# First MLP block of a fused attention and MLP kernel: from two halves of 256 columns to four token tiles of 128 columns

## The chip, the cores and the metric

One core of a Trainium2 chip. The metric is device time in microseconds (us) of one launch. Engines in the profile: PE (TensorE matmul; PEld its weight loads), DVE (VectorE), ACT (ScalarE), POOL (GpSimd), SP (SyncE, which here issues most DMAs).

## The reference

```python
def reference(A_x, A_wqkv, A_wo, B_x, B_w1, B_w3, B_w2):
    # _A_ref(x, wqkv, wo): q, k, v = x @ wqkv, 32 heads of 32; each position attends to
    #   itself and 7 earlier ones, 2 apart; softmax; then @ wo
    # _B_ref(x, w1, w3, w2): (silu(x @ w1) * (x @ w3)) @ w2
    x = A_x                       # 1 x 2048 x 1024, bfloat16
    xn = _layernorm(x, axis=-1)
    s = _A_ref(xn, A_wqkv, A_wo)  # wqkv 1024 x 3072, wo 1024 x 1024
    g = _silu(_B_ref(xn, B_w1, B_w3, B_w2))   # w1, w3 1024 x 3584, w2 3584 x 1024
    return x + s * g
```

## The kernel before

The 2048 tokens are worked in 4 chunks of 512 (`CH`), each chunk of 4 token tiles of 128. A chunk needs its normalized tokens transposed: `xnT`, 128 partitions x 8 (`KT`, the slices of D) x 512 tokens. With `xnT` as the moving operand, the weights being the stationary one, PE makes gate and up of 14 blocks of 256 features (`w1`, `w3` tiles of 512 KB each), q, k and v, and then multiplies by `w2` and `wo`. DVE does the windowed attention beside this in pieces that the list `side` hands out with estimated costs. The schedule is manual: each engine's instructions stand in the order in which the code issues them, and each engine's queue is worked in that order.

The change is in the start of chunk 0 (lines 524 to 598), where no earlier work covers the normalization. Tiles of tokens are `x0[0..3]`. The loads of tiles 0 and 1 come in halves from SP and ACT (L112, L113), those of 2 and 3 from SP (L115), then six weight tiles (`load_w`, L167) and the raw q/k/v weights (L500), all on SP's queue. `take_w` pops the first loaded weight tile; `w1f` and `w3f` are the first two.

PE first runs 13 dummy matmuls (L521). For each tile DVE makes statistics of two halves (`bn`: L204 twice, aggregate L552), ACT the root (`std`, L532), DVE the reciprocal and the normalize in place (`norm0`, L535 and L207). Tile 2's statistics are not made by DVE but by ACT: a sum (L560), its negative mean (L561) and mean (L563), and a Square with a sum (L570). PE transposes the normalized tile in two halves of four 128x128 pieces (`pe_transpose`, L543) into PSUM; ACT copies the first half and DVE the second into `xnT` (`copy_in`, L547). `bring0` does transposes and copies of one tile.

Then PE makes the first block's four PSUM tiles `gu[0..3]`, each 128 features x 512 tokens: gate and up for two groups of 128 features (`k // 2` is the group, `k % 2` chooses w1 or w3). `part0(k, h)` (L581) fills 256 of the 512 columns with 8 matmuls (L584), so half 0 needs tiles 0 and 1, half 1 tiles 2 and 3. The order on PE before: transposes of tiles 0 and 1; `part0` of k = 0, 2, 1 in half 0; transposes of tile 2; k = 3 in half 0; transposes of tile 3; k = 0 to 3 in half 1. After that come two more weight loads on SP, which wait until `part0` is done with `w1f` and `w3f`, two `gate_up` (Silu on ACT L245, product on DVE L247), and copies that permute the raw q/k/v weights (`permute`, L507). Then PE goes on with the blocks fb = 1, 2 and q, k, v (`proj_group`, L273), and with fb = 3 to 13 (`up_block`, L258), `down_half` (L447) and `wo_proj` (L416).

PSUM has eight banks: `psum_mm` six, `psum_aux` two. Transposes of tiles 0 to 2 use `psum_mm`, of tile 3 `psum_aux`, as `gu` is allocated after the transposes of tiles 0 and 1.

Of the kernel before, what the change touches and what calls it, by code (L numbers as in the profile page):

```python
# [10 lines left out]
ACTF = mybir.ActivationFunctionType  # L11
# [34 lines left out]
def kernel(  # L46
# [11 lines left out]
    nc = tc.nc  # L58
    P = 128
    S, D, F = 2048, 1024, 3584  # L60
# [15 lines left out]
    scale = float(Dh) ** -0.5  # L76
# [11 lines left out]
    psum_mm = ctx.enter_context(tc.tile_pool(name="psum_mm", bufs=6, space=bass.MemoryType.PSUM))  # L88
    psum_aux = ctx.enter_context(tc.tile_pool(name="psum_aux", bufs=2, space=bass.MemoryType.PSUM))
# [20 lines left out]
    x0 = [xp.tile([P, D], BF16, tag="x", name=f"x0_{st}") for st in range(NST)]  # L110
# [3 lines left out]
    for st in range(2, NST):  # L114
# [10 lines left out]
        out=ident[:], in_=ident[:], compare_op=ALU.not_equal, fill=1.0,  # L125
# [5 lines left out]
        out=maskb[:], in_=maskb[:], compare_op=ALU.is_ge, fill=-1.0e9,  # L131
# [22 lines left out]
    def load_w():  # L154
        item = next(w_next, None)
        if item is None:
            return
        kind, i = item
        wt = wstream.tile([P, KT, 2 * P], BF16, tag="w")
        if kind == "q":  # L160
            src, dst = wperm[:, :, 2 * i:2 * i + 2, :].rearrange("kt kp tj p -> kp kt (tj p)"), wt[:]
        elif kind == "2":
            src = w2_r[:, i * 4:(i + 1) * 4, 512:1024]
            dst = wt[:].rearrange("p a b -> p (a b)").rearrange("p (i n) -> p i n", n=512)
        else:
            src, dst = (w1_r if kind == "1" else w3_r)[:, :, i * 256:(i + 1) * 256], wt[:]
        nc.sync.dma_start(out=dst, in_=src)  # L167
        w_tiles.append((item, wt if kind != "2" else dst))

    def take_w(item):  # L170
        got, wt = w_tiles.popleft()
        assert got == item, (got, item)
        return wt
# [29 lines left out]
    def half_stats(x_t, stats, i):  # L203
        nc.vector.bn_stats(out=stats[:, i, :], in_=x_t[:, i * 512:(i + 1) * 512])  # L204

    def normalize(x_t, mean, rstd):
        nc.vector.tensor_scalar(  # L207
            out=x_t[:], in0=x_t[:], scalar1=mean, scalar2=rstd, op0=ALU.subtract, op1=ALU.mult,
        )
# [299 lines left out]
    V, A = nc.vector.tensor_copy, nc.scalar.copy  # L509
# [14 lines left out]
    mv0 = [small.tile([P, 2], FP32, tag="mv0", name=f"mv0_{st}") for st in range(NST)]  # L524
    rs0 = [small.tile([P, 1], FP32, tag="rs0", name=f"rs0_{st}") for st in range(NST)]
    st0 = [small.tile([P, 2, nc.vector.BN_STATS_DIM], FP32, tag="st0", name=f"st0_{st}") for st in range(NST)]
    tot = small.tile([P, 1], FP32, tag="tot", bufs=1)
    nm = small.tile([P, 1], FP32, tag="nm", bufs=1)
    junk = ep.tile([P, D], BF16, tag="gt", bufs=5, name="junk")

    def std(st):
        nc.scalar.activation(out=rs0[st][:], in_=mv0[st][:, 1:2], func=ACTF.Sqrt, bias=eps_t[:], scale=1.0)  # L532

    def norm0(st):
        nc.vector.reciprocal(out=rs0[st][:], in_=rs0[st][:])  # L535
        normalize(x0[st], mv0[st][:, 0:1], rs0[st][:])

    def pe_transpose(st, half):
        pool, tag = (psum_mm, "mm") if st < 3 else (psum_aux, "aux")
        tp = pool.tile([P, 4, P], BF16, tag=tag, name=f"tp{st}_{half}")  # L540
        for k in range(4):
            kt = half * 4 + k
            nc.tensor.transpose(tp[:, k, :], x0[st][:, kt * P:(kt + 1) * P], ident[:])  # L543
        return tp

    def copy_in(tp, st, half, eng):
        eng(out=xnT[:, half * 4:(half + 1) * 4, st * P:(st + 1) * P], in_=tp[:])  # L547

    def bn(st):
        half_stats(x0[st], st0[st], 0)  # L550
        half_stats(x0[st], st0[st], 1)
        nc.vector.bn_aggr(out=mv0[st][:], in_=st0[st][:])  # L552

    def bring0(st):
        tps = [pe_transpose(st, half) for half in range(2)]
        copy_in(tps[0], st, 0, A)
        copy_in(tps[1], st, 1, V)

    bn(0)
    nc.scalar.activation(out=junk[:], in_=x0[2][:], func=ACTF.Identity, accum_out=tot[:])  # L560
    nc.scalar.mul(out=nm[:], in_=tot[:], mul=-1.0 / (32.0 * D))  # L561
    std(0)
    nc.scalar.mul(out=mv0[2][:, 0:1], in_=tot[:], mul=1.0 / D)  # L563
    bn(1)
    norm0(0)
    std(1)
    norm0(1)
    bring0(0)
    bring0(1)
    nc.scalar.activation(  # L570
        out=junk[:], in_=x0[2][:], func=ACTF.Square, bias=nm[:], scale=1.0 / 32.0, accum_out=mv0[2][:, 1:2],
    )
    std(2)
    bn(3)
    std(3)
    norm0(2)
    norm0(3)
    w1f, w3f = take_w(("1", 0)), take_w(("3", 0))
    gu = [psum_mm.tile([P, CH], FP32, tag="mm", name=f"gu0_0_{k}") for k in range(4)]

    def part0(k, h):  # L581
        i, wt, cs = k // 2, (w1f if k % 2 == 0 else w3f), slice(h * 256, (h + 1) * 256)
        for kt in range(KT):
            nc.tensor.matmul(  # L584
                gu[k][:, cs], lhsT=wt[:, kt, i * P:(i + 1) * P], rhs=xnT[:, kt, cs],
                start=(kt == 0), stop=(kt == KT - 1),
            )

    for k in (0, 2, 1):
        part0(k, 0)  # L590
    bring0(2)
    part0(3, 0)
    bring0(3)
    for k in range(4):
        part0(k, 1)
    load_w()
    load_w()
    hts = [gate_up(gu[0], gu[1])]
# [40 lines left out]
    for t in range(3):  # L639
# [8 lines left out]
        for half in range(2):  # L648
            nc.sync.dma_start(
                out=wperm[half * 4:(half + 1) * 4, :, t * NJ:(t + 1) * NJ, :].rearrange("kt kp j p -> kp kt (j p)"),  # L650
                in_=pmh[t, half].rearrange("kp kt j p -> kp kt (j p)"),
# [80 lines left out]
```

## Time and profile before

| What | Value |
|---|---|
| Runs | 820.09, 820.98, 830.97 us |
| Median | 820.98 us |
| Profiled execution: its time | 819.93 us |
| Profiled execution: its span | 818.2 us |
| PE busy | 808.8 us (99%) |
| First matmul of `part0` (L584) | 9.45 us |
| First matmul of the block after it (L273) | 17.94 us |

Times within the profile count from the span's start. In the timeline a row is: start, busy time, engine, line, operation, output<-input, shape, count, and in brackets the idle time of the engine before it with what ended it. Matmuls are pipelined: a row of several runs from the first start to the last (modelled) end, so the pitch of one is less than its length. In the chain of waits a row is start, length, what; it is followed back from the last instruction, each step to what released it. The six weight tiles and the raw weights are DMAs; their issue on SP's queue and their landing are different times.

### The profile page before, as it was taken

What the parts mean: (1) busy time and instruction counts of PE and PEld (TensorE: products, weight loads), DVE (VectorE), ACT (ScalarE), POOL (GpSimd) and SP (SyncE); (2) the same over time, 40 slices, a digit from 0 to 9 for tenths busy, and PEclk for the clock granted to TensorE, in tenths of its full rate; (3) what the DMA queues carried; (4) which work ended last, traced back from release to release, by engine and by line L of the source; (5) the groups of instructions that cost most, each with busy time, mean ns of one, the idle gap of its engine ahead of it and who ended that gap; (6) DMA issues with size and microseconds to landing.
All of it is one profiled execution on the core that took longest, in us unless ns stands there. A gap on an engine that the chain in (4) does not pass through costs nothing.

```text
span 818.2 us, 9549 instructions
## 1 busy us (share of the span) xinstructions
PE 808.8 (99%) x3817; PEld 372.5 (46%) x3817; DVE 481.4 (59%) x489; ACT 206.1 (25%) x319; POOL 95.3 (12%) x176
## 2 busy tenths in 40 slices
PE   8999999999999999999999999999999999999997
PEld 5444444444444444444444444444444444444444
DVE  6619947693229765692224968489111695759432
ACT  6552133011432132101133213310223321311120
POOL 0000041301100223000110030400000004130010
PEclk9999999999999999999999999999999999999999
DMA  9992698795454786879255588869925548696810
GB/s 289 347 371 74 195 211 194 167 307 180 130 149 140 219 193 182 180 197 307 87 180 153 144 221 181 196 134 230 295 92 180 152 133 203 167 210 144 255 51 26
DMA packets 221085, 152.69 MB, mean 187 GB/s; under 512 B 19568, under 2 KB 209136, under 8 KB 221040
## 3 DMA queue, kind: packets, MB, share of 16 engines
q1 hardware_dynamic: 214224, 135.55, 60.8%
q0 software_dynamic: 6528, 16.26, 8.1%
q8 instruction: 30, 0.49, 0.2%
q10 hardware_dynamic: 288, 0.26, 0.1%
q14 instruction: 15, 0.12, 0.1%
HBM read 130.02 MB, written 10.49 MB: 172 GB/s over the span
## 4 chain that ended last, share of the span: by engine, by line
PE 97%; DMA 2%; ACT 0%; DVE 0%; SPq 0%; issue 0%
PE gu L258 45%; PE ps_qkv L273 20%; PE acc L447 19%; PE ps_wo L416 7%; PE acc L483 3%; DMA wt<-in_B_w_dram 2%; PE gu L273 2%; PE gu L584 1%; DMA x<-in_A_x_dram 0%; PE tp L543 0%; ACT xnT L547 0%; ACT junk L560 0%; SPq L112 0%; DVE x L207 0%; DVE gt L433 0%
## 5 line engine op out<-in xcount | busy, mean ns | idle before, releaser
L258 PE MATMUL gu<-xnT_next,wt 128*128 128x512 bf16 x1344 | 290.6, 379 | 0.0
L258 PEld LDWEIGHTS <-wt 128*128 128x128 bf16 x1696 | 166.0, 98 | 200.1
L447 PE MATMUL acc<-wt,ht 128*128 128x512 bf16 x784 | 170.7, 379 | 1.3 <-DMA wt<-in_B_w_dram 1.3
L247 DVE TENSOR_TENSOR ht<-sg,gu 128x512 bf16<-128x512 bf16 x112 | 75.8, 680 | 92.1 <-PE gu L258 67.6
L245 ACT ACTIVATE sg<-gu 128x512 bf16<-128x512 f32 x112 | 65.9, 597 | 247.7 <-PE gu L258 232.8
L273 PE MATMUL ps_qkv<-xnT_next,wt 128*128 128x512 bf16 x576 | 124.8, 379 | 0.0
L303 DVE TENSOR_TENSOR prod<-qT,kT 128x4096 bf16<-128x4096 bf16 x32 | 73.1, 2285 | 86.4 <-ACT kT L277 86.3
L447 PEld LDWEIGHTS <-ht 128*128 128x128 bf16 x784 | 76.7, 98 | 94.1 <-issue 1.8
L273 PEld LDWEIGHTS <-wt 128*128 128x128 bf16 x640 | 62.6, 98 | 75.3
L433 DVE TENSOR_TENSOR gt<-gt,s_sb 128x512 f32<-128x512 f32 (+1 forms) x33 | 22.2, 674 | 122.0 <-ACT gt L427 63.3
L258 PE MATMUL gu<-xnT,wt 128*128 128x512 bf16 x352 | 76.1, 379 | 0.0
L333 POOL DMA_DIRECT2D L<-E x64 | 37.1, 587 | 295.0 <-DVE E L318 190.1
L385 DVE TENSOR_TENSOR pv<-Pr,vT 128x4096 bf16<-128x4096 bf16 x28 | 63.2, 2283 | 0.0
L314 DVE TENSOR_TENSOR prod<-prod 128x2048 bf16<-128x2048 bf16 x64 | 61.1, 955 | 1.4
L416 PE MATMUL ps_wo<-wo,oT 128*128 128x512 bf16 x256 | 55.9, 379 | 0.0
L427 ACT ACTIVATE gt<-acc 128x512 f32<-128x512 f32 (+1 forms) x33 | 19.3, 584 | 141.1 <-PE acc L447 119.6
L374 POOL DMA_DIRECT2D Pr<-pb x64 | 36.8, 583 | 107.6 <-DVE pb L367 101.9
L273 PE MATMUL ps_qkv<-xnT,pm 128*128 128x512 bf16 x192 | 41.6, 379 | 0.0
L435 POOL DMA_DIRECT2D out_dram<-o_t x28 | 15.3, 545 | 209.4 <-DVE o_t L434 204.9
L416 PEld LDWEIGHTS <-oT 128*128 128x128 bf16 x256 | 25.0, 98 | 30.2
L420 ACT CAST s_sb<-ps_wo 128x512 bf16<-128x512 f32 x32 | 18.7, 585 | 77.9 <-PE ps_wo L416 77.9
L396 DVE TENSOR_TENSOR oT<-oT,pv 128x4096 bf16<-128x4096 bf16 x16 | 36.6, 2288 | 0.3
(67 smaller groups left out, 371.4 us busy)
## 6 DMA issues: line engine op xcount, KB each, us to landing
wt<-in_B_w_dram SPq DMA_DIRECT2D x168, 512.0 KB, 4.6
wt<-wperm SPq DMA_DIRECT2D x36, 512.0 KB, 5.4
wo<-in_A_wo_dram SPq DMA_DIRECT2D x32, 256.0 KB, 9.2
raw<-in_A_wqkv_dram SPq DMA_DIRECT2D x6, 1024.0 KB, 10.2
wperm<-pm SPq DMA_DIRECT2D x6, 1024.0 KB, 9.4
L<-E POOLq DMA_DIRECT2D x64, 64.0 KB, 5.8
Pr<-pb POOLq DMA_DIRECT2D x64, 64.0 KB, 4.2
xres<-in_A_x_dram POOLq DMA_DIRECT2D x4, 1024.0 KB, 6.9
```

Source lines behind the costliest of these rows:

```text
L245: nc.scalar.activation(out=sg[:], in_=g_ps[:], func=ACTF.Silu)
L247: nc.vector.tensor_mul(ht[:], sg[:], u_ps[:])
L258: nc.tensor.matmul(ps[:], lhsT=wt[:, kt, i * P:(i + 1) * P], rhs=xnT[:, kt, :], start=(kt == 0), stop=(kt == KT - 1),)
L273: nc.tensor.matmul(ps[:], lhsT=lhs(kt), rhs=xnT[:, kt, :], start=(kt == 0), stop=(kt == KT - 1))
L303: nc.vector.tensor_mul(prod, qT[:], kT[:, :, o:o + CH])
L314: nc.vector.tensor_add(prod[:, 0:n, :], prod[:, 0:n, :], prod[:, n:2 * n, :])
L333: nc.gpsimd.dma_start(out=L4[sq * 32:(sq + 1) * 32, r, :, :], in_=E[r * 32:(r + 1) * 32, :, sq * P:(sq + 1) * P],)
L374: nc.gpsimd.dma_start(out=Pr[r * 32:(r + 1) * 32, :, sq * P:(sq + 1) * P], in_=pb[sq * 32:(sq + 1) * 32, :, :],)
L385: nc.vector.tensor_mul(dst, Pr[:, w, :].unsqueeze(1).to_broadcast([P, NJ, CH]), vT[:, :, o:o + CH])
L396: nc.vector.tensor_add(a, a, b)
L416: nc.tensor.matmul(ps[:], lhsT=oT[:, j, st * P:(st + 1) * P], rhs=was[dh][:, j, :], start=(j == 0), stop=(j == NJ - 1),)
L447: nc.tensor.matmul(accs[st][:], lhsT=hts[f][:, st * P:(st + 1) * P], rhs=w2t[:, i, :], start=(f == 0), stop=(f == FT - 1),)
```

## The change

- `part0(k, st)` now fills the 128 columns of one token tile: 128 matmuls of 128 columns replace 64 of 256, the accumulation over the 8 slices unchanged.
- `gu` and the first two weight tiles are taken before the first transposes, and the transposes of tiles 1 and 2 use `psum_aux`, of 0 and 3 `psum_mm`.
- The order is written out anew. PE: transposes of tile 0; k = 0, 2 (w1) of tile 0; transposes of tile 1; k = 1, 3 (w3) of tile 0; k = 0, 2, 1, 3 of tile 1; transposes of tile 3; of tile 2; k = 0 to 3 of tile 3; k = 0 to 3 of tile 2.
- ACT: the root of tile 0 stands ahead of the sum over tile 2; the copy of tile 0 ahead of the root of tile 1; tile 2's mean and Square follow the copy of tile 1; the root of tile 3 ahead of that of tile 2.
- DVE: the halves of the statistics of tiles 1 and 3 are put between other jobs: tile 1's first half ahead of the normalize of tile 0, its second after it; tile 3's first half after the normalize of tile 1, its second after the copy of tile 1. Tile 3 is normalized ahead of tile 2.
- SP's and POOL's instructions keep their order. No instruction of ACT or DVE is added or removed.

```diff
     def pe_transpose(st, half):
-        pool, tag = (psum_mm, "mm") if st < 3 else (psum_aux, "aux")
+        pool, tag = (psum_mm, "mm") if st in (0, 3) else (psum_aux, "aux")
...
-    bn(0)
-    nc.scalar.activation(out=junk[:], in_=x0[2][:], func=ACTF.Identity, accum_out=tot[:])
-    nc.scalar.mul(out=nm[:], in_=tot[:], mul=-1.0 / (32.0 * D))
-    std(0)
-    nc.scalar.mul(out=mv0[2][:, 0:1], in_=tot[:], mul=1.0 / D)
-    bn(1)
-    norm0(0)
-    std(1)
-    norm0(1)
-    bring0(0)
-    bring0(1)
-    nc.scalar.activation(
-        out=junk[:], in_=x0[2][:], func=ACTF.Square, bias=nm[:], scale=1.0 / 32.0, accum_out=mv0[2][:, 1:2],
-    )
-    std(2)
-    bn(3)
-    std(3)
-    norm0(2)
-    norm0(3)
     w1f, w3f = take_w(("1", 0)), take_w(("3", 0))
     gu = [psum_mm.tile([P, CH], FP32, tag="mm", name=f"gu0_0_{k}") for k in range(4)]
 
-    def part0(k, h):
-        i, wt, cs = k // 2, (w1f if k % 2 == 0 else w3f), slice(h * 256, (h + 1) * 256)
+    def part0(k, st):
+        i, wt, cs = k // 2, (w1f if k % 2 == 0 else w3f), slice(st * P, (st + 1) * P)
         for kt in range(KT):
             nc.tensor.matmul(
                 gu[k][:, cs], lhsT=wt[:, kt, i * P:(i + 1) * P], rhs=xnT[:, kt, cs],
                 start=(kt == 0), stop=(kt == KT - 1),
             )
 
-    for k in (0, 2, 1):
-        part0(k, 0)
-    bring0(2)
+    half_stats(x0[0], st0[0], 0)
+    half_stats(x0[0], st0[0], 1)
+    aggr(0)
+    std(0)
+    half_stats(x0[1], st0[1], 0)
+    norm0(0)
+    tp0 = bring0(0)
+    nc.scalar.activation(out=junk[:], in_=x0[2][:], func=ACTF.Identity, accum_out=tot[:])
+    nc.scalar.mul(out=nm[:], in_=tot[:], mul=-1.0 / (32.0 * D))
+    half_stats(x0[1], st0[1], 1)
+    aggr(1)
+    copy_in(tp0[0], 0, 0, A)
+    copy_in(tp0[1], 0, 1, V)
+    std(1)
+    norm0(1)
+    part0(0, 0)
+    part0(2, 0)
+    tp1 = bring0(1)
+    half_stats(x0[3], st0[3], 0)
+    copy_in(tp1[0], 1, 0, A)
+    copy_in(tp1[1], 1, 1, V)
+    part0(1, 0)
     part0(3, 0)
-    bring0(3)
-    for k in range(4):
+    nc.scalar.mul(out=mv0[2][:, 0:1], in_=tot[:], mul=1.0 / D)
+    nc.scalar.activation(
+        out=junk[:], in_=x0[2][:], func=ACTF.Square, bias=nm[:], scale=1.0 / 32.0, accum_out=mv0[2][:, 1:2],
+    )
+    half_stats(x0[3], st0[3], 1)
+    aggr(3)
+    std(3)
+    std(2)
+    norm0(3)
+    norm0(2)
+    for k in (0, 2, 1, 3):
         part0(k, 1)
+    tp3 = bring0(3)
+    copy_in(tp3[0], 3, 0, A)
+    copy_in(tp3[1], 3, 1, V)
+    tp2 = bring0(2)
+    copy_in(tp2[0], 2, 0, A)
+    copy_in(tp2[1], 2, 1, V)
+    for st in (3, 2):
+        for k in range(4):
+            part0(k, st)
     load_w()
     load_w()
```

`bring0` now only transposes and returns the two PSUM tiles; `aggr(st)` is the aggregate that was the last line of `bn`.

More of the change, by code (lines that the diff above doesn't have):

```diff
@@ L547, in copy_in, with aggr @@
         eng(out=xnT[:, half * 4:(half + 1) * 4, st * P:(st + 1) * P], in_=tp[:])
-    def bn(st):
-        half_stats(x0[st], st0[st], 0)
-        half_stats(x0[st], st0[st], 1)
+    def aggr(st):
         nc.vector.bn_aggr(out=mv0[st][:], in_=st0[st][:])
     def bring0(st):
-        tps = [pe_transpose(st, half) for half in range(2)]
-        copy_in(tps[0], st, 0, A)
-        copy_in(tps[1], st, 1, V)
-    bn(0)
-    nc.scalar.activation(out=junk[:], in_=x0[2][:], func=ACTF.Identity, accum_out=tot[:])
-    nc.scalar.mul(out=nm[:], in_=tot[:], mul=-1.0 / (32.0 * D))
-    std(0)
-    nc.scalar.mul(out=mv0[2][:, 0:1], in_=tot[:], mul=1.0 / D)
-    bn(1)
-    norm0(0)
-    std(1)
-    norm0(1)
-    bring0(0)
-    bring0(1)
-    nc.scalar.activation(
-        out=junk[:], in_=x0[2][:], func=ACTF.Square, bias=nm[:], scale=1.0 / 32.0, accum_out=mv0[2][:, 1:2],
-    )
-    std(2)
-    bn(3)
-    std(3)
-    norm0(2)
-    norm0(3)
+        return [pe_transpose(st, half) for half in range(2)]
     w1f, w3f = take_w(("1", 0)), take_w(("3", 0))
     gu = [psum_mm.tile([P, CH], FP32, tag="mm", name=f"gu0_0_{k}") for k in range(4)]
-    def part0(k, h):
-        i, wt, cs = k // 2, (w1f if k % 2 == 0 else w3f), slice(h * 256, (h + 1) * 256)
+    def part0(k, st):
+        i, wt, cs = k // 2, (w1f if k % 2 == 0 else w3f), slice(st * P, (st + 1) * P)
         for kt in range(KT):
```

## The prediction

> **What bounds the kernel now.** I read the busy shares first, then the chain of waits in order of time, then the waits of TensorE (PE), then the first 20 us row by row.
>
> ```profile
> PE 808.8 (99%) x3817; PEld 372.5 (46%) x3817; DVE 481.4 (59%) x489; ACT 206.1 (25%) x319; POOL 95.3 (12%) x176
> ```
>
> PE is busy for 99% of the span. The chain of waits, cut to its first 60 us (start, length, what):
>
> ```profile
> 1.69 3.61 DMA x<-in_A_x_dram
> ...
> 7.12 0.56 DVE x L207
> ...
> 7.72 0.62 PE tp L543 x8
> ...
> 9.45 2.78 PE gu L584 x24
> 12.23 0.45 PE tp L543 x8
> 12.68 0.87 PE gu L584 x8
> 13.55 0.24 PE tp L543 x4
> ...
> 13.81 0.59 ACT xnT L547
> ...
> 14.45 3.65 PE gu L584 x32
> 18.10 13.81 PE gu L273 x64
> 31.91 28.27 PE ps_qkv L273 x131
> ```
>
> From 14.45 us on the chain stays on PE. So one number decides: the start of the first L273 matmul, the one after the changed region. The timeline has it at 17.94 us (the chain prints ends, so 18.10). What is won or lost before that moves the rest as a block, unless a wait on a DMA swallows it. PE's waits (in total, times, longest) are few. The first row lies after 160 us, the second is in the region of the change:
>
> ```profile
> PE acc L447 <- DMA wt<-in_B_w_dram: 1.3, 2, 1.0
> ...
> PE gu L584 <- ACT xnT L547: 0.9, 2, 0.5
> ```
>
> The prices of a matmul come from the timeline of PE, 13.3 to 18.3 us, and the time at which the first weights land comes from the DMA issues with their time to landing:
>
> ```profile
> 13.39 0.61 PE L543 MATMUL tp<-ident,x 128*128 128x128 bf16 x8
> 14.45 3.65 PE L584 MATMUL gu<-xnT,wt 128*128 128x256 bf16 x32 [0.45 <-ACT xnT L547]
> 17.94 0.59 PE L273 MATMUL gu<-xnT,wt 128*128 128x512 bf16 x2
> ```
> ```profile
> wt<-in_B_w_dram SPq DMA_DIRECT2D x1, 512.0 KB, 5.2
> ```
> ```profile
> wt<-in_B_w_dram SPq DMA_DIRECT2D x1, 512.0 KB, 6.5
> ```
>
> The two loads are issued at 2.64 and 3.11 us, so the w1 tile lands at 7.84 and the w3 tile at 9.61. Groups give a mean length of 272 ns for a 256-column matmul, 219 ns for a transpose. Pitch (start to start) of a 256-column pair of weight load and matmul: (3.65 - 0.27) / 31 = 0.109 us. Pitch of a 128-column pair: (0.61 - 0.22) / 7 = 0.056 us, from transposes, each of which also loads new weights.
>
> **The change part by part**, all on the clock of the profiled execution.
>
> *Columns.* 64 matmuls of 256 columns (64 x 0.109 = 6.98 us) become 128 of 128 columns, each with its own weight load (128 x 0.056 = 7.17). So PE gets 0.19 us more work, provided that a weight load hides behind a 128-column matmul as it does behind a transpose. No row shows such a matmul with wt. From below I bound it by the transposes' 0.056; from above by the duration of one weight load (group row: 98 ns), as if none of it overlapped. I take 0.056, the row of the same shape and pairing.
>
> The Trainium skill, in "TensorE: Matmul & The Clock Gate", section Back-to-back issue gap, speaks against this: it says that in a stream of weight-load and matmul pairs a 128-column matmul sustains only about 81 ns, against 56 ns alone. By 81 ns the sum below would come out at a loss of about 1.8 us. The same sentence gives 131 ns for 512 columns, and here 64 of them take 13.81 us, 216 ns each; as its other end misses this trace, I stay with the row.
>
> *Tile 0 first.* In the old order statistics of tiles 0 and 1, then three small ScalarE (ACT) jobs around a sum over tile 2 (5.32 to 6.61), stand before the root of tile 0, whose normalize (VectorE, DVE) starts at 7.12. Now the root follows the statistics of tile 0 directly: aggregate ends at 4.92 + 0.21 = 5.13, root 0.28 -> 5.45, but DVE first does half of tile 1's statistics (5.04 to 5.68), then reciprocal and normalize (0.20 + 0.55) -> 6.42; transposes at 6.47 (0.05 after, as 7.67 -> 7.72). ACT's copy starts 0.44 later (7.72 -> 8.16) at 6.91 and lasts 0.59, behind the sum over tile 2 that was pushed back by about 0.05 and is done by about 6.75. DVE's copy comes 0.66 after the transposes, behind the rest of tile 1's statistics: about 7.15 to 7.6. So tokens of tile 0 are there at 7.65, and now the weights are late: w1 lands at 7.84. PE starts at 7.86 instead of 9.45.
>
> *Parts of tile 0 and 1.* Two groups with w1: 16 x 0.056 -> 8.76. Tile 1 is normalized by about 8.5 (its root waits on ACT for the copy of tile 0, 7.50, and ends at about 7.75; + 0.20 + 0.55), later than the 8.33 of before, but ahead of PE. Its transposes: 8 x 0.056 -> 9.21. Next are the w3 groups, and w3 lands at 9.61, so PE waits 0.4 us: start at 9.63. Nothing but weight loads and matmuls is queued behind. Then 16 + 32 pairs without a wait (tile 1's copies: 8.76 + 0.44 + 0.59 = 9.79): 48 x 0.056 = 2.69 -> 12.32.
>
> *Tiles 3 and 2.* ACT: after the copy (9.79) the mean 0.19, the Square 1.05 and its read-out 0.19, then the root of tile 3, 0.28 -> about 11.45; DVE 0.03 + 0.20 + 0.55 -> 12.2, which is 0.1 before PE is free. Tile 2 follows 0.66 later (7.12 -> 7.78): 12.9. PE: transposes of tile 3 at 12.32, then from transposes to the first matmul of that tile 1.06 us, as 13.39 -> 14.45: 13.38. The transposes of tile 2 (12.95 to 13.4) fit into that gap. Then 64 x 0.056 = 3.58 -> 16.96.
>
> *Sum.* First L273 matmul at 16.96 instead of 17.94: 0.98 us gained. In words: old 32 pairs after the last copy cost 3.49, the new 64 cost 3.58; the gain is that the last wait on a copy begins at 12.32 instead of 13.39, less 0.09.
>
> *Costed at nothing.* PSUM: transposes 1 and 2 now go through the two aux banks, 0 and 3 through two of the six mm banks. Every tile that reuses a bank comes after matmuls that already waited for that bank's copies. SP's queue: the same loads in the same order; the two loads after part0 wait for its last matmuls (0.5 us in the queue's waits), now earlier, and queue behind 4 MB of raw weights. POOL: unchanged. ACT's table load (14.41, 1.28 us) now comes after the copy of tile 2, about 14.1, ending 15.4, before the first Silu has its inputs at about 15.8. Permutes: they wait for raw weights (23.40), which PE does not hasten; the last one for q ends at 26.50 + 2.03 = 28.53 and q starts at 31.75, so 3.2 us of cover against 0.98 wanted.
>
> **Between the ends.** Best: PE never waits after 7.86: (128 + 24) x 0.056 = 8.51 -> 16.37, a gain of 1.57. Worst: 0.098 a pair: 7.86 + 1.57 + 0.45 = 9.88, + 48 x 0.098 = 14.58, + 1.06 + 64 x 0.098 = 21.91, a loss of 3.97. ACT's small jobs in the step on tiles 3 and 2 may run 0.3 us longer than their rows; that would cost 0.2.
>
> **The rivals.**
> - *A, the other side: the dearer pair.* Place: part0's 112 pairs behind the wait on w3. 9.63 + 112 p + 1.06 passes 17.94 at p = 0.065 us. Above that the kernel is slower: up to 820.98 + 3.97 = 824.95. For it: weight loads last 98 ns and the moving side is now half as long; against it: transposes at 0.056 with such a load each. Chance 0.12.
> - *B, the gain is swallowed.* The two stalls on w2 tiles after 160 us become longer by what PE is early: 820.98. Against it: in the chain the load of the first begins at 159.72, where PE's stretch from 149.33 (10.37 long) ends, so the load is released by PE and moves with it. Chance 0.13.
> - *C, it doesn't do what it says.* Matmuls do not start "as soon as the tile is normalized": weights hold w1 and w3. If the weights land 0.5 us later than before, the path from 9.63 moves by as much: gain 0.48, 820.5. Against it: the loads before them are the same. Chance 0.07.
>
> **How the numbers follow.** The forecast (0.68): the profiled execution goes from 819.93 (span 818.2 and 1.73 around it) to 818.95. The median of the runs shown is 820.98, 1.05 above that execution, and the same gain makes it 820.0. Its own range: gain of 1.57 to 0.3, and runs that spread from 820.09 to 820.98: 818.5 to 821.0 (one of the three runs shown, 830.97, stands apart; a median is not moved by one such). With B and C, and the smaller half of A, the range is 818.5 to 822.3, which leaves out under 2 in 10. About 2%, 16 us, is what a measurement of this kernel can tell from no change; no case here reaches that, so within 2% gets 0.97; 0.02 for slower (A with something more, or a disturbed median), 0.01 for faster.
>
> **What would show it.** Right: first part0 matmul at about 7.86, a PE wait on w3 of about 0.4 us, 128-column pairs at 0.056 pitch (8 of them in about 0.61), one wait on ACT's copy before the last 64, first L273 matmul at about 17.0, and all later stretches as long as before. Wrong: a pitch over 0.065, a wait of PE on DVE's normalize of tile 3 or 2, or a wait on w2 at 160 us longer by a microsecond.

## The result, and the profile after

Over 20 runs of each kernel the median went from 821.32 to 823.83 us: ratio 1.0032, 95% interval 1.0016 to 1.0048. The changed kernel is slower by about 2.5 us, where 1 us less was forecast. (Ratios, here and below, are over the runs in the chip's faster state alone, one of before at 1128.94 us left out, and are not the quotients of the medians.) Its profiled execution took 823.57 us (span 821.8), against 819.93 (818.2) before.

The start did what was forecast in kind, with a smaller lead. The timeline of PE in the changed kernel, first 18 us:

```profile
6.37 0.62 PE L543 MATMUL tp<-ident,x 128*128 128x128 bf16 x8 [0.36 <-DVE x L207]
8.43 1.07 PE L561 MATMUL gu<-xnT,wt 128*128 128x128 bf16 x16 [1.44 <-DMA wt<-in_B_w_dram]
9.33 0.61 PE L543 MATMUL tp<-ident,x 128*128 128x128 bf16 x8
10.23 2.85 PE L561 MATMUL gu<-xnT,wt 128*128 128x128 bf16 x48 [0.29 <-DMA wt<-in_B_w_dram]
12.93 1.06 PE L543 MATMUL tp<-ident,x 128*128 128x128 bf16 x16
13.99 3.73 PE L561 MATMUL gu<-xnT,wt 128*128 128x128 bf16 x64
17.56 0.81 PE L273 MATMUL gu<-xnT,wt 128*128 128x512 bf16 x2
```

The rows show the two waits for weights, the last 64 pairs at (3.73 - 0.22) / 63 = 0.056 us each, and the next block 0.38 us ahead of before (17.94). So the whole loss, 3.6 us of span and 0.4 of lead, arose later. PE's waits over the whole run (total, times, longest):

```profile
PE acc L447 <- DMA wt<-in_B_w_dram: 2.4, 2, 1.5
PE gu L561 <- DMA wt<-in_B_w_dram: 1.7, 2, 1.4
PE acc L447 <- DVE ht L247: 1.5, 2, 0.9
...
PE gu L258 <- DVE ht L247: 0.7, 1, 0.7
```

The first was 1.3 before, the two on DVE's `ht` did not exist. (The chain of waits is no help here: one matmul record in about 50 is missing from this trace, and each gap breaks the chain. I compared the starts of the weight loads instead, all of which are recorded.) Matching load by load from the end of the program, the changed kernel runs 0.38 us ahead up to 160 us; then the difference grows by 1.19 at 166.87 of the old clock (a wait on a w2 tile), 0.71 at 352.48, 1.11 at 363.70 (w2), 0.87 at 548.46 and 1.28 more up to 552.77 (DVE's `ht`), and falls by 1.15 at 565.14, where before had its own wait. From 20 us on, the instructions of every engine are the same in both programs, in the same order. The first of these losses, in PE's timeline from 154 to 169 us, before:

```profile
166.87 2.32 PE L447 MATMUL acc<-wt,ht 128*128 128x512 bf16 x10 [0.27 <-DMA wt<-in_B_w_dram]
```

and in the changed kernel:

```profile
167.68 1.67 PE L447 MATMUL acc<-wt,ht 128*128 128x512 bf16 x7 [1.47 <-DMA wt<-in_B_w_dram]
```

The two stretches that end in a wait on w2 hold a DMA that no line of the kernel issues and that they lack before. The DMA view by queue, 159 to 168 us, before:

```profile
q1 hardware_dynamic: 3185, 1.59, 70.6%
q0 software_dynamic: 272, 1.05, 38.2%
```

and the same stretch of the changed kernel:

```profile
q1 hardware_dynamic: 2877, 1.28, 67.4%
q0 software_dynamic: 272, 1.05, 34.8%
q8 instruction: 1, 0.02, 0.6%
```

and 355 to 367 us of the changed kernel, where before shows no q8 row either:

```profile
q8 instruction: 1, 0.02, 0.5%
issues: line engine op xcount, KB each, median us to landing
wt<-in_B_w_dram SPq DMA_DIRECT2D x4, 512.0 KB, 5.1
xres<-in_A_x_dram POOLq DMA_DIRECT2D x1, 1024.0 KB, 8.4
```

q8 carries 30 packets of 16 KB in both profiles, about 27.7 us apart: 128 pairs of weight load and 512-column matmul at 0.216 us. 16 KB are 256 instructions if one has 64 bytes, so I take these to be PE's own instructions: 30 packets of 128 pairs are 3840, and the trace of before has 3817 matmuls. The Trainium skill, "Runtime: NRT & Kernel Launch", section Instruction fetch mechanics, says just this: an engine's instructions are fetched in 16 KiB blocks of 256 over a DMA queue of its sequencer. It calls the cost mostly hidden. The 16 KB and the distance of the packets agree with it; what they cost is the subject of the experiments. The change adds 64 matmuls and 64 weight loads at the start, 128 instructions, so every later packet should come 64 pairs, 13.8 us, earlier in the work. Packets in the trace of before: 148.5, 179.5, 344.1, 372.5, 540.2, 567.8 us; in the changed kernel 139.6, 164.7, 192.4, 330.2, 359.2, 524.0, 555.8.

### The profile page after: what moved, and what is told of

It is laid out like the page before. It is cut to its first block, busy times and chain, and to the rows that moved or that the text cites. A ratio compares the mean times of both kernels' runs of the same rounds, so it can differ in the third digit from the quotient of the medians.

```text
span 821.8 us, 9603 instructions
## 1 busy us (share of the span) xinstructions
PE 805.8 (98%) x3807; PEld 373.3 (45%) x3881; DVE 481.2 (59%) x489; ACT 205.7 (25%) x319; POOL 95.7 (12%) x176
## 4 chain that ended last, share of the span: by engine, by line
PE 35%; DVE 12%; DMA 7%; issue 4%; POOL 1%; ACT 1%; DVEq 0%; ACTq 0%; POOLq 0%
PE acc L447 13%; PE ps_qkv L273 8%; PE gu L258 6%; PE ps_wo L416 5%; DMA Pr<-pb 4%; PE acc L483 3%; DVE pv L385 2%; DVE prod L303 2%; DMA L<-E 2%; DVE ht L247 2%; DVE prod L314 1%; POOL Pr L374 1%; DMA wt<-in_B_w_dram 1%; DVE oT L396 1%; DVE stats L204 1%
## 5 line engine op out<-in xcount | busy, mean ns | idle before, releaser
L273 PE MATMUL ps_qkv<-xnT_next,wt 128*128 128x512 bf16 x565 | 124.2, 379 | 0.6
L273 PEld LDWEIGHTS <-wt 128*128 128x128 bf16 x640 | 62.6, 98 | 75.3
L273 PE MATMUL ps_qkv<-xnT,pm 128*128 128x512 bf16 x188 | 41.4, 379 | 0.2
L435 POOL DMA_DIRECT2D out_dram<-o_t x28 | 15.3, 547 | 203.6 <-DVE o_t L434 198.3
L396 DVE TENSOR_TENSOR oT<-oT,pv 128x4096 bf16<-128x4096 bf16 x16 | 36.6, 2288 | 0.3
```

What stands on the lines that cost most here:

```text
L273: nc.tensor.matmul(ps[:], lhsT=lhs(kt), rhs=xnT[:, kt, :], start=(kt == 0), stop=(kt == KT - 1))
L396: nc.vector.tensor_add(a, a, b)
```

## The experiments

Theories: *phase* or *lead* (PE arrives earlier, and its paced loads then collide), *plain size* (each added instruction costs), *spread* (single programs differ by so much anyway), and, after the first four runs, *fetch* (where the instruction packets fall). In the table, PE instructions are counted against before; ratios are to runs of before on the same chip.

| Kernel | PE instructions | Median us, before beside it | Ratio, 95% interval |
|---|---|---|---|
| before again | 0 | 820.61, 821.18 | 0.9990, 0.9976 to 1.0004 |
| before, 8 matmuls less | -16 | 820.75, 821.18 | 0.9997, 0.9980 to 1.0015 |
| before, 32 pairs more | +64 | 823.96, 820.51 | 1.0048, 1.0026 to 1.0069 |
| before, 64 pairs more | +128 | 824.23, 821.18 | 1.0037, 1.0023 to 1.0051 |
| changed, last half as before | +64 | 821.77, 820.51 | 1.0018, 1.0008 to 1.0027 |
| changed | +128 | 823.83, 821.32 | 1.0032, 1.0016 to 1.0048 |
| changed, 4 dummies behind part0 | +136 | 822.76, 821.18 | 1.0026, 1.0002 to 1.0050 |
| changed, 32 pairs more | +192 | 821.31, 820.51 | 1.0011, 0.9994 to 1.0027 |
| changed, 48 pairs more | +224 | 819.95, 821.45 | 0.9977, 0.9954 to 1.0000 |
| changed, 64 pairs more | +256 | 819.76, 820.51 | 0.9988, 0.9978 to 0.9999 |
| changed, 80 pairs more | +288 | 821.68, 821.45 | 1.0008, 0.9987 to 1.0030 |

**Before, again.** No edit.

> The kernel before, unchanged, as a program of its own. It shows how far two programs that are the same differ, and where on PE their times part in the trace. Spread theory (the 0.3% is the scatter of single programs, whose stalls on w2 tiles after 160 us fall differently in each run): the median may differ from before by 2 us either way, and the profile shows stalls after 160 us that add up to between 1 and 5 us. Phase theory and size theory: median within 0.7 us of before, the profile's PE waits after 160 us near the 1.3 us of before.

No difference that can be measured: in this one repeat, spread between programs does not make 0.3%. Its profile had 0.2 us of waits on w2, not 1.3, and the first L273 matmul at 19.43 instead of 17.94: both ends of that single profile of before scatter by over 1 us, in opposite ways.

**Changed, lead taken back.**

```diff
             part0(k, st)
+    pad = psum_aux.tile([P, CH], FP32, tag="aux", name="pad_ps")
+    for _ in range(4):
+        nc.tensor.matmul(pad[:], lhsT=warm[:, 0:P], rhs=warm[:, 0:CH], start=True, stop=True)
     load_w()
```

> The changed kernel with 4 dummy matmuls of 512 columns (4 x 0.216 = 0.86 us) on PE between part0 and the next block; they write to a PSUM tile of their own. Phase theory (PE's earlier arrival moves its paced weight loads against the attention's transfers, and the waits after 160 us grow by more than the gain): with the lead taken back, the time falls to that of before, about 821.3, in spite of 0.86 us more work. Size theory (64 more matmuls and weight loads in the program, wherever they stand, cost later): 823.8 + 0.9 = 824.7. Spread theory: anywhere from 820.5 to 825.

1.0026: still slower than before, so taking the lead back did not bring back the time. It lies between the two expectations and its interval is wide; alone it settles nothing. Its next block starts at 17.86 in its profile, 0.08 us before that of before.

**Before, with as many PE instructions as the changed kernel.** The dummies at the start only keep PE busy until the tokens come.

```diff
-    busy(warm, 13)
+    for _ in range(77):
+        nc.tensor.matmul(wps[:, 0:P], lhsT=warm[:, 0:P], rhs=warm[:, 0:P], start=True, stop=True)
```

> The kernel before with its 13 dummy matmuls of 512 columns at the start replaced by 77 of 128 columns, so that PE has exactly as many instructions as in the changed kernel, while they end before the first transposes (about 7.3 us) and nothing else moves. Size theory: as slow as the changed kernel, 823.8. Phase theory: as before, 821.3.

1.0037: the whole loss, without any of the change. PE's timeline shows the dummies done before the transposes, which wait for DVE as before; the next block starts at 18.39, inside what runs of before show (17.94 and 19.43):

```profile
1.23 5.88 PE L524 MATMUL warm_ps<-warm 128*128 128x128 bf16 x77 [1.23 <-DVE warm L119]
8.18 1.27 PE L544 MATMUL tp<-ident,x 128*128 128x128 bf16 x16 [1.07 <-DVE x L207]
...
18.39 0.81 PE L273 MATMUL gu<-xnT,wt 128*128 128x512 bf16 x2
```

Its waits are of the changed kernel's kind:

```profile
PE acc L447 <- DMA wt<-in_B_w_dram: 2.5, 3, 1.4
...
PE acc L447 <- DVE ht L247: 0.4, 1, 0.4
```

and in 159 to 168 us it has an instruction packet too, with the two w2 loads issued there slower (median 7.8 us to landing; 6.4 before, for three, and 6.7 in before again, for two):

```profile
q8 instruction: 1, 0.02, 1.2%
issues: line engine op xcount, KB each, median us to landing
xres<-in_A_x_dram POOLq DMA_DIRECT2D x1, 1024.0 KB, 7.0
wt<-in_B_w_dram SPq DMA_DIRECT2D x2, 512.0 KB, 7.8
```

**Before, 0.87 us earlier by leaving work out.**

```diff
-        for kt in range(KT):
+        n = KT - 2 * h
+        for kt in range(n):
```

(`stop` moves to `kt == n - 1`.)

> The kernel before with 8 matmuls left out: in the second half of part0 two of the 8 slices of D are left out for each of the four tiles, so PE is 8 x 0.109 = 0.87 us earlier from then on, and gate and up of the first block lack these slices for 256 tokens. Phase theory: the lead alone makes it slower than before, about 823 to 824, though it has less work. Size theory: the lead is kept, 821.3 - 0.9 = 820.4. Spread theory: either.

0.9997: a lead alone does not make it slower. That it isn't 0.9 us faster either lies within its interval. Its profile has a wait of 0.8 us on w2 near 170 us with no packet there (151.0 and 184.8 us).

**Changed, with another 64 pairs: 256 instructions, one whole packet.** The test of fetch against plain size. The edit is that of the 77 dummies, on the changed kernel.

> The changed kernel with its 13 dummy matmuls of 512 columns replaced by 77 of 128, that is 128 more PE instructions than the changed kernel and 256 more than before. The traces show 16 KB instruction packets for PE at about every 27.7 us; 16 KB are 256 instructions of 64 bytes, so 128 matmuls and their weight loads. Fetch theory (the 128 added instructions move the packets 13.8 us ahead of the work, into the stretches where the transfers of w2, transposes and attention are tight: 164.7, 359.2, 555.8 us, where before had 148.5 and 179.5, 344.1 and 372.5, 540.2 and 567.8): 256 added instructions put the packets back where before has them, and the time falls to 820.5 to 821.5 although the program has grown again. Plain size theory (each added matmul costs): 826 to 827. The later end of the dummy matmuls (7.3 us) costs at most 0.5 us, as w1 lands at 7.8 to 8.4.

819.76 against 820.51: the program has grown again and is now faster than before, by 0.75 us (ratio 0.9988, 0.9978 to 0.9999). Plain size falls. The 77 dummies end at 8.26 us here, not at 7.3, and the next block starts at 18.09, so this profile has not kept the lead. The packets are back where before has them (148.7, 179.6, 343.6, 372.6, 540.2, 567.9 us), the two stretches have no q8 row, and PE's waits are again those of before:

```profile
PE acc L447 <- DMA wt<-in_B_w_dram: 1.1, 2, 0.9
PE gu L562 <- ACT xnT L548: 0.5, 1, 0.5
```

Queues in 159 to 168 us:

```profile
q1 hardware_dynamic: 3182, 1.59, 69.4%
q0 software_dynamic: 272, 1.05, 39.1%
issues: line engine op xcount, KB each, median us to landing
wt<-in_B_w_dram SPq DMA_DIRECT2D x3, 512.0 KB, 6.3
xres<-in_A_x_dram POOLq DMA_DIRECT2D x1, 1024.0 KB, 6.3
```

**Changed, with 32 more pairs** (45 dummies).

> The changed kernel with 45 dummy matmuls of 128 columns: 192 PE instructions more than before, packets 20.7 us ahead of those of before (about 158.8, 351.8, 547). Fetch theory: another time than the changed kernel's, between 820.5 and 824, as one of the three tight stretches (159 to 168) still has its packet. Plain size theory: 825.

1.0011: far from plain size (825), and inside the range of fetch, which was wide, though not for the reason given. The stretch at 160 us lost only 0.43 us with its packet at 156.4. The profile's larger losses, on its own clock, are 1.08 us at 353.89, in a wait on DVE's `ht` (the packet is at 352.2), and 1.47 at 366.58, in a wait on w2 with no packet within 12 us.

**Before, with 32 more pairs** (45 dummies).

> The kernel before with 45 dummy matmuls of 128 columns: 64 PE instructions more, packets 6.9 us ahead (about 172.6, 365.6, 560.9). Fetch theory: between 821 and 824, with a longer stall on w2 at 565 at least. Plain size theory: half of the 3 us that 128 instructions cost, 822.7.

1.0048, at the top of what fetch allowed and over twice the loss that plain size gave. Its profiled execution was its slowest run, 830.64 us, so it doesn't show what made the median. It has the packet at 559.7 and then this:

```profile
573.22 3.14 PE L447 MATMUL acc<-wt,ht 128*128 128x512 bf16 x7 [6.82 <-DMA wt<-in_B_w_dram]
```

**The early half of the change alone**: tiles 2 and 3 in 256 columns once both are there (`part0` gets the number of tiles as a third argument).

```diff
-    for st in (3, 2):
-        for k in range(4):
-            part0(k, st)
+    for k in range(4):
+        part0(k, 2, 2)
```

> The changed kernel with tiles 2 and 3 done in 256-column matmuls once both are there, as before: the early half of the change alone, 64 PE instructions more than before (packets as in the one with 32 more dummies). Fetch theory: its time less the lead of the early half, about 0.5 us below that run. Plain size theory: 822.5 - 0.5.

1.0018 against 1.0048 of the kernel before at the same count: 0.3% less, 2.2 us by the medians, more than the 0.5 expected (their intervals just touch). Its largest loss, on its own clock, is 1.28 us at 756.77, in a wait on DVE's `ht`, 4 us after a packet at 752.8.

**Changed, with 48 more pairs** (61 dummies).

> The changed kernel with 61 dummy matmuls of 128 columns: 224 PE instructions more than before, so packets 3.5 us later in the work than in before (about 152 and 183, 347.6 and 376, 543.7 and 571.3), and the dummies end before the weights land, so the whole lead of the early start is kept. Fetch theory: no packet in the stretches 159 to 168, 355 to 367, 557 to 568, so faster than before by the lead, 819.3 to 820.3. Lead theory (the lead is what costs, and 64 more dummies helped only by taking 0.5 us of it back): 822.5 to 824. Plain size theory: 825 to 826.

819.95 against 821.45: faster, as fetch had it, and clear of the 822.5 that the lead theory gave. The next block starts at 17.83 in its profile, so part of the lead is kept (17.56 in the changed kernel, 17.94 before). The interval, 0.9954 to 1.0000, just reaches no difference. PE waited for w2 0.8 us in all. The run with 4 dummies behind `part0` has nearly the same start, 17.86, and 88 instructions less: 1.0026 (1.0002 to 1.0050) against 0.9977 here. The intervals don't overlap, so the start of the block alone doesn't set the time.

**Changed, with 80 more pairs** (93 dummies).

> The changed kernel with 93 dummy matmuls of 128 columns: 288 PE instructions more than before, 256 + 32, so packets 3.5 us ahead of those of before (about 145 and 176, 340.6 and 369, 536.8 and 564.4), and the dummies end about 0.9 us later than with 77. Fetch theory: a packet at the end of the third stretch, 820.5 to 822.5. Lead theory: no lead is left, so as before, 820.5. Plain size theory: 827.

1.0008: no gain, as fetch had it (its packet at 564.8 is at the end of the third stretch, 557 to 568 us, as expected), but its profile, 817.8 us of span, shows no loss there. The lead theory gave about as much; this run does not tell them apart.

## Why the prediction was wrong

- *PE bounds; the start of the first L273 matmul decides.* The start came 0.38 us earlier, as forecast in kind, but "moves the rest as a block" did not hold: the rest became 4.0 us longer (3.6 of span and 0.4 of lead), for the reason under *Columns*.
- *128-column pairs at 0.056 us.* Right: 0.056. Rival A had no part in the loss. The 81 ns for such a stream that the Trainium skill gives in "TensorE: Matmul & The Clock Gate", section Back-to-back issue gap, does not hold here.
- *Weights late, w1 at 7.84, w3 at 9.61; PE waits 0.4 us.* Right in kind. They landed about 0.6 us later in that execution, so PE waited 1.44 and then 0.29, and the lead was 0.38 instead of 0.98. But the execution of before that I calculated from was early: other programs with its order have the first L273 matmul at 18.39, 19.18 and 19.43. By the medians, the changed kernel gains 0.75 us where the packets stand as before (+256).
- *One wait on the copies before the last 64; the transposes of tile 2 fit into it.* Right: 12.93 to 13.99 is 1.06 us.
- *Columns: "So PE gets 0.19 us more work".* This is the step that failed. The added matmuls were priced on PE's array alone and, under "Costed at nothing", the number of PE's instructions does not appear. The Trainium skill's page "Runtime: NRT & Kernel Launch", section Instruction fetch mechanics, would have told that 256 instructions make a packet. The price of the 128 instructions was not 0.19 us but about 3 us (824.23 against 821.18 for the same number with none of the change), not on PE's array but in waits on w2 tiles and, after transfers `Pr<-pb`, on DVE.
- *Rival B, the gain is swallowed.* The right place, the waits after 160 us, and the wrong cause and size: not the lead but the count moved them, and they took more than the lead. The sign that the prediction named, a wait on w2 at 160 us longer by a microsecond, did come: 0.27 became 1.47.

What is shown: the time depends on the number of PE instructions ahead, and not steadily. On the kernel before, 64 cost 0.5% and 128 0.4%; the changed kernel, slower by 0.3% with 128, is not slower with 224 or 256, and those with 256 have the packets where before has them.

What is only argued: that the packet itself delays the transfers beside it. The twelve traces say this of the three stretches:

- 159 to 168 us: in the three traces with a packet there (changed, changed with 4 dummies behind `part0`, before with 64 pairs more) PE waits 1.1 to 1.9 us for w2, in the other nine 0.2 to 0.8.
- 355 to 367 us: the wait on w2 is 0.9 to 1.4 us in three traces (changed, changed with 32 pairs more, before with 64 pairs more) and at most 0.3 in the others, whether a packet is in the stretch or not. The three are those in which POOL issues its 1 MB load `xres` latest, at 356.6 to 357.2 us; the others issue it by 356.4. In the changed kernel that issue follows an `oT` of DVE (L396), whose attention had waited 7.3 us for `Pr<-pb`, against 4.8 before. So if a packet has a part in this wait, it is by way of the attention.
- 557 to 568 us: the seven traces with a packet there wait 0 to 6.8 us for w2, the five without 0 to 0.2.

No run changed a packet and nothing else, so something else that goes with the count, such as where the program lies in memory, is not excluded.

## What to carry to other kernels

When a kernel is bound by PE but has stretches in which its loads arrive just in time, a change in the number of its instructions can cost or gain more than the edit itself, as here: compare with a control that has the same count and none of the edit. Before a verdict on a change of 1 us in 800, try it at two or three counts (here by dummy matmuls where PE idles anyway). With 64 more dummies the edit gains about 0.75 us against before (by the interval 0.1 to 1.8); without them it loses.

## What was not expected of the hardware

- One packet of 16 KB at 18.6 us took 1.19 us, and one part of each later load stayed behind by about as much. In the trace of before, the raw weight tile that lands at 23.38 us has 15 of its 16 parts by 22.12 and the last 1.25 us later; the next six loads land with the same lag of 1.24 to 1.26 us. That the late part is the one that shares a DMA engine with the packet is my reading; the trace doesn't name the engines. The lag is not always that long: after the changed kernel's packet at 15.3 us (1.20 us) it was 0.38.
- A similar lag stands beside the attention's transfers in the changed kernel: from 500 to 549 us the last of 16 parts comes up to 2.6 us after the others (on `Pr<-pb` up to 1.7), and DVE's wait for `Pr<-pb` in that chunk grows from 4.8 to 8.8 us. Packets are at 500.6 and 524.0, but the lag is 0.93 us already at 499.23, so they are not its only cause. The w2 tile that ends the wait of 1.47 us lands whole, first to last part within 0.22 us. From 495 to 560 us of before, DVE's wait was

```profile
DVE oT L385 <- DMA Pr<-pb: 4.8, 1, 4.8
```

and of the changed kernel, where PE then waits twice for DVE's `ht` (0.9 and 0.7 us):

```profile
DVE oT L385 <- DMA Pr<-pb: 8.8, 1, 8.8
```

- In the execution with the wait of 6.82 us, the granted clock was 0.60 from 573 to 580 us, and the matmuls after it ran at about 0.43 us each instead of 0.216.
